# Which DMAs a kernel waits for before it ends: every semaphore, or the stores alone

## The chip, the cores and the metric

The kernel runs on one core of one Trainium2 chip. The metric is the time of one execution on the device, in microseconds; lower is better.

## The reference

Four residual layers over x of shape (1, 2048, 512) in bf16: twice a linear attention of 32 heads with softmax feature maps, each followed by a gated unit with ReLU.

```python
def reference(A_x, A_wqkv, A_w_phi, A_wo, B_x, B_W_gate, B_W_up, B_W_down):
    ...  # _A_ref: attention; _B_ref: gate * (gate > 0) * up, then W_down
    x = A_x
    x = x + _A_ref(_layernorm(x, axis=-1), A_wqkv, A_w_phi, A_wo)
    x = x + _B_ref(_layernorm(x, axis=-1), B_W_gate, B_W_up, B_W_down)
    x = x + _A_ref(_layernorm(x, axis=-1), A_wqkv, A_w_phi, A_wo)
    x = x + _B_ref(_layernorm(x, axis=-1), B_W_gate, B_W_up, B_W_down)
    return x
```

## The kernel before

A small scheduler in Python orders all operations, gives each DMA a semaphore and emits one instruction stream for each engine. Cuts are marked with `...`.

```python
    def prepare(self):
        ...
        ring = soft = 0
        for o in self.sequence:
            ...
            if o.dma:
                if e == "pool":
                    o.stream = ("d", self.n_dma_sems - 4 + soft % 4)
                    soft += 1
                else:
                    o.stream = ("d", ring % (self.n_dma_sems - 4))   # a ring of 60
                    ring += 1
                if o.stream in last_of:
                    deps.append(last_of[o.stream])
            ...
            cnt[o.stream] += 1
            o.cnt = cnt[o.stream]
        self.final = cnt

    def emit(self, e, eng, sems, dsems):
        for o in self.seq[e]:
            ...  # waits of the operation, the operation, its increment
        if e == "sp":
            for s, c in self.final.items():
                if isinstance(s, tuple) and c:
                    eng.wait_ge(dsems[s[1]], 16 * c)
```

The output leaves in 17 stores. Sixteen are issued by ScalarE's queue; the last 128 columns of the last tile are issued by SyncE:

```python
            if last:
                op(OUT_Q if w == 512 else "sp" if n0 else "act", lambda e, n0=n0, n1=n1: e.dma_start(outv[:, t:t + 1, n0:n1], x_sb[:, t:t + 1, n0:n1]), ..., dma="store", ...)
```

A wait that is written with no operation after it is attached by the compiler to the next instruction, here the branch that leaves the block. That branch keeps the first wait of the list; the others become wait instructions of up to two semaphores ahead of it, paired from the middle of the list outward, so that the list's end is waited for last. That is read from the records of this kernel: the branch carries the first of the 62 semaphores, and the last instruction the 62nd together with the second.

The softmax here doesn't subtract the row's maximum and nothing guards it: scores larger than these inputs give would overflow.

## Time and profile before

| | before |
|---|---|
| time, first three runs | 390.05, 390.68, 390.74 us |
| profiled execution: time, span | 389.32, 387.52 us |
| SyncE issues the last store | 384.80 us after the span's start |
| that store has landed | 1.51 us after its issue |
| SyncE's branch / its drain | 2.32 / 2.50 us after its issue |
| end of the span | 2.73 us after its issue |

The lower four rows are the tail; they come from the trace's single records of instructions and semaphore increments. A DMA has landed when its semaphore has had the sixteenth increment; the drain is the instruction that SyncE executes next after the branch. I measure every tail from the start of SyncE's last store issue, because that takes out whatever happened earlier in the run. The lines of the profile stand in the prediction below.

### The profile page before, as it was taken

The page shows a single profiled execution, that of the slowest core. Times are in us where ns is not written, and L with a number is a line of the kernel's source. Part 1 is how long each engine was busy: PE and PEld are TensorE (multiplying, and loading weights), DVE is VectorE, ACT ScalarE, POOL GpSimd, SP SyncE. Part 2 cuts the span into 40 slices and gives each one's busy share as a digit, 9 for nine tenths or more (in the row PEclk, how much of TensorE's full clock was granted, in tenths as well). Part 3 has the DMA queues.
Part 4 walks back from the last instruction along what each step waited for, and adds up shares of the span by engine and source line. Part 5 has one row for each costly group of instructions (what it writes and reads, how often), then busy time and mean ns, then how long its engine had stood idle before and what let it go on. Part 6 is the DMA issues. An engine that isn't in the chain of part 4 may idle for free.

```text
span 387.5 us, 6658 instructions
## 1 busy us (share of the span) xinstructions
PE 377.9 (98%) x2430; PEld 214.0 (55%) x2471; DVE 294.7 (76%) x646; ACT 195.0 (50%) x609; POOL 57.4 (15%) x129
## 2 busy tenths in 40 slices
PE   8999899999999999999999999999999999999996
PEld 7545565787554544444444467577565554454443
DVE  7999977999997886663798986899867773643442
ACT  6999859664253236243255765875343344024210
POOL 1377201213112000000000000232201020100000
PEclk9999999999999999999999999999999999999999
DMA  8451951233232222010030100022331231210101
GB/s 258 152 102 37 308 184 30 43 61 63 55 79 44 44 54 41 15 27 2 7 62 2 27 3 2 14 42 55 70 82 29 54 61 35 69 27 14 42 14 54
DMA packets 60592, 22.89 MB, mean 59 GB/s; under 512 B 51760, under 2 KB 60304, under 8 KB 60560
## 3 DMA queue, kind: packets, MB, share of 16 engines
q1 hardware_dynamic: 57440, 19.35, 22.2%
q10 hardware_dynamic: 2832, 2.08, 1.7%
q0 software_dynamic: 288, 1.05, 0.8%
q8 instruction: 19, 0.31, 0.3%
q14 instruction: 13, 0.11, 0.1%
HBM read 8.44 MB, written 2.10 MB: 27 GB/s over the span
## 4 chain that ended last, share of the span: by engine, by line
PE 76%; DVE 10%; ACT 9%; DMA 2%; issue 1%; POOL 1%; SPq 0%; POOLq 0%
PE pb L872 32%; PE pb L926 17%; PE pb L842 5%; PE pb L726 5%; PE pb L673 4%; PE pb L711 4%; PE pb L746 3%; ACT phik L684 3%; PE pb L779 3%; PE pb L900 2%; ACT expq L730 2%; PE pb L928 2%; DVE phik L702 2%; DVE stats L615 2%; DVE t L816 1%
## 5 line engine op out<-in xcount | busy, mean ns | idle before, releaser
L879 ACT ACTIVATE gate<-pb 128x512 bf16<-128x512 f32 (+1 forms) x100 | 51.0, 511 | 77.0 <-PE pb L872 74.2
L880 DVE TENSOR_TENSOR hT<-gate,pb 128x512 bf16<-128x512 bf16 (+1 forms) x100 | 56.8, 576 | 39.4 <-PE pb L872 36.9
L872 PE MATMUL pb<-yT,Wu 128*128 128x512 bf16 (+1 forms) x396 | 82.6, 336 | 0.2
L872 PE MATMUL pb<-yT,Wg 128*128 128x512 bf16 (+1 forms) x393 | 81.6, 336 | 0.5
L926 PE MATMUL pb<-Wd,hT 128*128 128x512 bf16 (+2 forms) x322 | 75.5, 372 | 0.5
L872 PEld LDWEIGHTS pb<-yT,Wu 128*128 128x128 bf16 x400 | 38.8, 98 | 30.6 <-DVE x_sb L845 0.6
L872 PEld LDWEIGHTS pb<-yT,Wg 128*128 128x128 bf16 x400 | 38.6, 98 | 29.3 <-DVE t L821 0.3
L926 PEld LDWEIGHTS pb<-Wd,hT 128*128 128x128 bf16 x330 | 31.7, 98 | 35.2
L615 DVE BATCH_NORM_STATS2 stats<-x_sb 128x6 f32<-128x512 bf16 x64 | 43.2, 686 | 1.7 <-DMA x_sb<-in_A_x_dram 1.0
L730 ACT ACTIVATE expq<-pb 128x512 bf16<-128x512 f32 x64 | 35.2, 617 | 8.9 <-PE pb L726 8.9
L684 ACT ACTIVATE phik<-pb 128x512 bf16<-128x512 f32 x64 | 35.6, 612 | 6.6 <-PE pb L673 6.6
L816 DVE TENSOR_TENSOR t<-pb,sm 128x384 bf16<-128x384 f32 x64 | 33.5, 549 | 1.4 <-POOL sm L806 1.2
L934 DVE TENSOR_TENSOR x_sb<-x_sb,pb 128x512 bf16<-128x512 bf16 (+2 forms) x33 | 21.9, 666 | 14.4 <-PE pb L928 14.4
L624 ACT ACTIVATE lnv<-mv,eps 128x1 f32<-128x1 f32 (+1 forms) x58 | 17.2, 305 | 29.7 <-DVE mv L616 29.4
L842 PE MATMUL pb<-wo,oT 128*128 128x512 bf16 x119 | 30.9, 379 | 1.0 <-DMA oT<-o 0.5
L641 DVE TENSOR_SCALAR y<-x_sb,mv,rstd 128x512 bf16<-128x512 bf16 x63 | 28.2, 462 | 4.0 <-ACT rstd L626 3.8
L711 PE MATMUL pb<-wv,yT 128*128 128x512 bf16 x124 | 30.7, 379 | 0.2
L726 PE MATMUL pb<-yT,Wqp 128*128 128x512 bf16 x124 | 30.6, 379 | 0.3
L673 PE MATMUL pb<-Wkp,yT 128*128 128x512 bf16 x120 | 30.2, 379 | 0.5 <-DMA yT<-y 0.3
L845 DVE TENSOR_TENSOR x_sb<-x_sb,pb 128x512 bf16<-128x512 bf16 x32 | 21.8, 680 | 11.3 <-PE pb L842 10.8
L793 ACT ACTIVATE sm<-pb 128x48 f32<-128x48 f32 (+1 forms) x96 | 16.5, 215 | 20.1 <-PE pb L779 19.9
L693 DVE TENSOR_REDUCE z<-phik 128x64 f32<-128x1024 bf16 x21 | 25.0, 1201 | 0.9 <-ACT phik L684 0.6
(81 smaller groups left out, 411.5 us busy)
## 6 DMA issues: line engine op xcount, KB each, us to landing
out_dram<-x_sb ACTq DMA_DIRECT2D x15, 128.0 KB, 1.7
Wg<-in_B_W_gate_dram SPq DMA_DIRECT2D x2, 640.0 KB, 6.6
Wu<-in_B_W_up_dram SPq DMA_DIRECT2D x2, 640.0 KB, 7.7
Wd<-in_B_W_down_dram SPq DMA_DIRECT2D x1, 1280.0 KB, 12.6
x_sb<-in_A_x_dram POOLq DMA_DIRECT2D x2, 512.0 KB, 4.5
yT<-y SPq DMA_TRANSPOSE x55, 2.5
Wd<-in_A_wqkv_dram SPq DMA_DIRECT2D x2, 256.0 KB, 3.0
Wd<-in_A_wqkv_dram SPq DMA_DIRECT2D x1, 512.0 KB, 5.2
```

Source lines behind the costliest of these rows:

```text
L615: op("dve", lambda e, t=t: e.bn_stats(stats[:, t, :], x_sb[:, t, :]), reads=[res("x", t)], writes=[res("st", t)], ii=600, lat=690, name=f" ...
L673: i = e.matmul(kt.ap(), src.ap()[:, ic, c0:c0 + 128], Wkp[:, ic, :], start=(ic == 0), stop=(ic == 3))
L684: op("act", lambda e, s=s: e.activation(ft.ap()[:, s, :], kt.ap(), ACT.Exp, scale=(1.0, -1.0)[s]), reads=[kr], writes=[fr2[s]], ii=477, la ...
L711: i = e.matmul(vt.ap(), src.ap()[:, ic, c0:c0 + 128], wv[:, ic, :], start=(ic == 0), stop=(ic == 3))
L726: i = e.matmul(qt.ap(), Wqp[:, ic, c * 128:(c + 1) * 128], src.ap()[:, ic, :], start=(ic == 0), stop=(ic == 3))
L730: op("act", lambda e, g=g: e.activation(es[g][0].ap(), qt.ap(), ACT.Exp, scale=(1.0, -1.0)[g]), reads=[qr], writes=[es[g][1]], ii=477, lat ...
L816: return e.tensor_tensor(tt_.ap()[:, b, 0:384].rearrange("p (c h d) -> p c h d", h=8, d=16), pt.ap()[:, 0:432].rearrange("p (c w) -> p c w ...
L842: i = e.matmul(wt.ap(), oT_.ap()[:, c, :], wo[:, c, :], start=(c == 0), stop=(c == 3))
L872: i = e.matmul(pt.ap()[:, 0:n], W[:, ic, fc * 128:(fc + 1) * 128], src.ap()[:, ic, a * 128:b * 128], start=(ic == 0), stop=(ic == 3))
L879: op("act", lambda e: e.activation(st_.ap()[:, 0:n], gt.ap()[:, 0:n], ACT.Relu), reads=[gr], writes=[sr], ii=110 + n * .72, lat=230 + n * ...
L880: op("dve", lambda e: e.tensor_tensor(ht.ap()[:, a * 128:b * 128], st_.ap()[:, 0:n], ut.ap()[:, 0:n], ALU.mult), reads=[sr, ur], writes=[h ...
L926: i = e.matmul(pt.ap()[:, 0:n1 - n0], hT[l, s, fc].ap()[:, c:c + 128], Wd[:, fc, n0:n1], start=(fc == 0), stop=False)
```

## The change

The loads and transposes have all been waited for by whoever used their data, so only the stores have nobody who waits for them. The change waits for those alone, in the order in which they are expected to land.

```diff
         if e == "sp":
-            for s, c in self.final.items():
-                if isinstance(s, tuple) and c:
-                    eng.wait_ge(dsems[s[1]], 16 * c)
+            for o in sorted((o for o in self.ops if o.dma == "store"), key=lambda o: o.end):
+                eng.wait_ge(dsems[o.stream[1]], 16 * o.cnt)
```

## The prediction

> **What bounds the kernel now.** I read the page first. TensorE is busy for 98% of the span, and the chain that ended last is made of its matmuls:
>
> ```profile
> span 387.5 us, 6658 instructions
> PE 377.9 (98%) x2430; PEld 214.0 (55%) x2471; DVE 294.7 (76%) x646; ACT 195.0 (50%) x609; POOL 57.4 (15%) x129
> ...
> PE 76%; DVE 10%; ACT 9%; DMA 2%; issue 1%; POOL 1%; SPq 0%; POOLq 0%
> ```
>
> The change touches nothing of that. It edits only the code that SyncE runs after its last DMA, so what counts is how the program ends. I therefore read the timeline from 384.4 us on (columns: start, duration, engine, line, operation):
>
> ```profile
> 383.86 0.91 DVE L934 TENSOR_TENSOR x_sb<-x_sb,pb 128x384 bf16<-128x384 bf16 x2 [1.11 <-PE pb L928]
> 384.22 0.22 PE L928 MATMUL pb<-Wd,hT 96*128 96x128 bf16 x1
> 384.45 0.34 ACTq L937 DMA_DIRECT2D out_dram<-x_sb  x1
> 384.80 0.38 SPq L937 DMA_DIRECT2D out_dram<-x_sb  x1
> ```
>
> The last matmul ends at 384.44, the last VectorE addition at 383.86 + 0.91 = 384.77, and SyncE issues the last of the 17 stores from 384.80 to 385.18. After that nothing computes, yet the span runs 2.3 us further, to 387.5. The time from issue to landing is in the list of DMA issues:
>
> ```profile
> out_dram<-x_sb ACTq DMA_DIRECT2D x1, 96.0 KB, 1.6
> out_dram<-x_sb SPq DMA_DIRECT2D x1, 32.0 KB, 1.5
> ```
>
> So the last two stores are down at about 384.45 + 1.6 = 386.1 and 384.80 + 1.5 = 386.3. In the trace's own semaphore records the sixteenth increments are at 386.08 and 386.30. The program is therefore not ended by its last store: 387.5 is 1.2 us later. Line 420 (the loop that the change replaces) and line 1001 (the end of the block) fill that stretch:
>
> ```profile
> L420 SPq EVENT_SEMAPHORE  x31: 17/28/28, 385.2 to 387.1; - x31
> ...
> L1001 SPq COMPARE_BRANCH  x1: 41/41/41, 387.1 to 387.1; - x1
> L1001 SPq DRAIN  x1: 13/13/13, 387.3 to 387.3; - x1
> ...
> L1001 DVEq DRAIN  x1: 328/328/328, 384.5 to 384.5; - x1
> L1001 ACTq DRAIN  x1: 152/152/152, 384.8 to 384.8; - x1
> ...
> L1001 POOLq EVENT_SEMAPHORE  x2: 17/17/17, 387.3 to 387.4; - x2
> L1001 SPq EVENT_SEMAPHORE  x1: 17/17/17, 387.5 to 387.5; - x1
> ```
>
> What to see: SyncE executes 31 wait instructions on one line, without a pause, from 385.2 to 387.1, then a branch and a drain; VectorE and ScalarE drained at 384.8 and 385.0. GpSimd's barrier instruction comes only after SyncE's drain, and the release of all engines ends the span. In the single records the first wait starts at 385.228, the last at 387.056, so (387.056 - 385.228) / 30 = 61 ns from one to the next, and the branch follows at 387.121. No wait in the row is longer than its neighbours: the two that carry the last stores' semaphores come up at 386.81 and 386.87, half a microsecond after those had landed. The tail is bound by SyncE's sequencer working through waits that are nearly all long satisfied.
>
> **What the Trainium skill says.** "Perfetto Trace Analysis", section "Sequencer-only Instruction (DRAIN, etc)", says that the profiler reports only the execution of such an instruction, while decode and semaphore wait lie outside. The trace agrees: 28 ns reported, 61 ns from start to start; I count with the 61. "Advanced Engine Details and Errata", section "Network/Comms", puts the reading of a semaphore by the sequencer at 50-100 ns. The records show two semaphores on 30 of the 31 instructions, so about 61 ns for two; the measurement decides. "DMA: Bandwidth & Descriptors", section "Anatomy of one DMA — SWDGE (gpsimd) path", describes about 2.0 us of fixed time, most of it the write receipt, for a software-issued DMA. These hardware-issued stores take 1.5 to 2.1 us, the last one 1.5 for 32 KB; it is the floor under the end whatever SyncE does.
>
> **The change part by part.** Removed: waits on 62 semaphores. The kernel makes 128 DMAs; SyncE and ScalarE share a ring of 60 semaphores, all used, and GpSimd's two loads have one each. 62 = 1 on the branch + 1 + 30 x 2, which is the 31 instructions plus the branch. Added: waits for the 17 stores alone. Following the kernel's own schedule (computed from the kernel before, which fixes it), the 17 stand on 17 different semaphores, so none can be merged away. By the same packing, one goes on the branch and 16 make 8 instructions. 31 - 8 = 23 instructions go; the page should count 6658 - 23 = 6635. Removed waits guard only loads and transposes, which their users wait for anyway, so the schedule of all five engines up to 385.18 is the same.
>
> The naive gain is 23 x 61 ns = 1.40 us. It can't all be had, because the landing steps in. The packing in the records is from the middle outward (first the 31st, then 32nd with 30th, and so on to the last with the second; the first in the list sits on the branch). I apply it to the 17 in the schedule's order of ends: the 16 after the first pair up from the middle, and the seventh instruction has the store that lands at 386.08, the eighth the one of 386.30. Step by step: start at 385.23 as before; six satisfied waits, 6 x 0.061, bring SyncE to 385.59; the seventh holds until 386.08; the eighth would be reached at about 386.14 and holds until 386.30. An update releases a waiting sequencer in about 0.02 us here (VectorE's last increment is at 384.78, SyncE's issue starts at 384.798), so the last wait starts at 386.32. The branch follows 0.065 later, as before (387.056 to 387.121): 386.385. Before it was 387.121, so the branch comes 0.736 us earlier. What follows (branch to drain 0.18, drain to end 0.22) is unchanged and moves with it.
>
> Sum: 1.40 us of waits removed, of which 0.66 becomes a wait for the landing; 0.74 us on the path. The profiled span should be 387.52 - 0.74 = 386.8, and the time 390.68 - 0.74 = 389.94. The three times before average 390.49, which would give 389.75; I put the point between, at 389.9.
>
> **The rivals.**
> - *The wait moves, but ends with the waits in the wrong place.* If the pairing put the last store's wait first, all seven other waits would follow its landing: 386.32 + 7 x 0.061 + 0.065 = 386.81, a gain of only 0.31 us: 390.4. For it: the order in the code is the modelled one, and the compiler permutes it. Against it: the permutation of the kernel before takes the ends of the list last, and the model's last two are the stores that landed last. The change's words promise the landing order; it needs only that the late ones come late.
> - *The landing was the end already, and the profile's row of waits is drawn out by the recording of each instruction.* Without a profile, 31 waits of 35 ns would end at 385.23 + 1.09 = 386.3 and the gain would vanish: 390.6. For it: all I have is a recorded run, and its time (389.32) is not that of the timed ones. Against it: the recorded run is the faster one, so recording does not visibly slow the kernel.
> - *The full 1.40 us*, 389.3, if the stores landed before the waits ran out. Against it: the landing at 386.30 is an event of the DMA, and the store's issue does not move.
> - *Something after the branch grows.* SyncE's program gets 23 instructions shorter and its end lies elsewhere in memory, so a late instruction fetch at the branch could eat some tenths: 390.0 to 390.4. The gap of 0.18 us between branch and drain may hold such a piece; the profile cannot say.
> - *TensorE's part changes.* Nothing in the change reaches it, but its chain is 98% of the time and 0.2% of it is as large as the gain.
>
> **Range and chances.** The mechanism can give 0 to 1.4 us, with 0.74 as the reading of the trace. The three timed runs lie 0.69 apart, as much as the gain. Adding half of that spread on either side of the point gives 389.2 to 390.6. A gain of 2% would be 7.8 us; the whole stretch from the last matmul to the end is 3.1 us, so faster by 2% is nearly excluded, and there is no added work on any path for a loss of 7.8 us. What is left, 1% each, is for a chip or state that differs.
>
> **What would show it right or wrong.** Right: the row of SyncE waits has 8 instructions instead of 31, starts at 385.2 and ends near 386.3; it has two visible stops, at the two last landings; the branch is at 386.4 and the span 386.8; every engine's busy time is as before. Wrong: a different count (packing); the last wait starting some multiples of 61 ns after the last landing (order); the branch-to-drain gap above 0.2 us (fetch); the span down 0.7 but the time not (recording). If the last stores were issued earlier or later than 384.45 and 384.80 by over 0.1 us, the difference is TensorE's, not the change's.

## The result, and the profile after

| | before | after |
|---|---|---|
| median of 6 runs | 390.19 us (389.88 to 390.74) | 389.31 us (388.85 to 389.79) |
| ratio | 1 | 0.9975, 95% interval 0.9962 to 0.9988 |
| SyncE's wait instructions | 31 | 8 |
| last store's landing after its issue | 1.505 us | 1.506 us |
| SyncE's branch after that issue | 2.323 us | 1.590 us |
| end of the span after that issue | 2.725 us | 1.993 us |

A ratio is the mean time of one kernel's fast runs over that of the other's of the same rounds, so not quite the ratio of the two medians. Here 0.9975 stands for 0.98 us; its interval, 0.47 to 1.48 us, holds the 0.73 us of the tail.

The head of the page of the kernel after, then the timeline of its end (start, duration, engine, line, operation):

```profile
span 388.0 us, 6635 instructions
```

```profile
385.65 0.34 ACTq L936 DMA_DIRECT2D out_dram<-x_sb  x1
385.99 0.38 SPq L936 DMA_DIRECT2D out_dram<-x_sb  x1
```

The wait instructions of its line 419, and the end of the block in its line 1000 (count; shortest, median and longest duration in ns; starts of the first and the last):

```profile
L419 SPq EVENT_SEMAPHORE  x8: 28/28/28, 386.4 to 387.5; - x8
```

```profile
L1000 SPq COMPARE_BRANCH  x1: 41/41/41, 387.6 to 387.6; - x1
L1000 SPq DRAIN  x1: 13/13/13, 387.8 to 387.8; - x1
```

Read against the prediction's lines: 31 has become 8, and 6658 records 6635 (both traces hold 2430 matmul records; the other eleven hold 2471). SyncE still starts to wait 0.43 us after it began to issue the last store (386.42 against 385.99). In the single records six waits follow each other at 59 to 74 ns, the seventh starts only with the landing of the last store but one, the eighth 16 ns after the last landing, and the branch 68 ns later.

But this profiled run's span is longer than the one of before, 387.99 against 387.52. The last store is issued 1.2 us later, and that happened at the beginning of the run. These are the transfers of the query weights in the two lists of DMA issues (size, time to landing), before and then after:

```profile
Wd<-in_A_wqkv_dram SPq DMA_DIRECT2D x1, 512.0 KB, 5.2
```

```profile
Wd<-in_A_wqkv_dram SPq DMA_DIRECT2D x1, 512.0 KB, 7.3
```

In the timeline of after the first transposes of these weights had to wait for them, and VectorE's second copy of the group after the transposes; the same copy in the timeline of before is the second fence:

```profile
10.49 0.62 PE L586 MATMUL pb<-ident,Wd 128*128 128x128 bf16 x8 [1.46 <-DMA Wd<-in_A_wqkv_dram]
...
10.92 0.42 DVE L477 COPY yT<-pb 128x512 bf16<-128x512 bf16 x1 [1.31 <-PE pb L586]
```

```profile
9.53 0.42 DVE L478 COPY yT<-pb 128x512 bf16<-128x512 bf16 x1
```

Is that the change's doing? Nothing before SyncE's last store differs in the two programs, and the 13 traces, in which that part of the program is the same but for one kernel that adds waits in SyncE's idle time, show the copy anywhere between 9.22 us and 10.92 us. In eleven of them it starts 0.48 us after the query weights have landed; in the two with the earliest landings (before and one_each) 1.20 and 0.57 us pass. Why the landings vary is not shown. From the copy to the last store's issue it is then 374.95 to 375.27 us in twelve of the traces. The thirteenth, order_alone, has 376.39 us; there the granted TensorE clock (a share of full speed) is 0.50 from 11 to 14 us, and 1.00 in the same window of all the others. So the arrival of the first loads spreads the times by more than the change moves them, and each tail has to be read by itself.

### The profile page after: what moved, and what is told of

It reads as the page before. It is cut to its first block, busy times and chain, and to the rows that moved or that the text cites. A ratio compares the mean times of both kernels' runs of the same rounds, so it can differ in the third digit from the quotient of the medians.

```text
span 388.0 us, 6635 instructions
## 1 busy us (share of the span) xinstructions
PE 378.6 (98%) x2430; PEld 214.7 (55%) x2471; DVE 294.8 (76%) x646; ACT 194.9 (50%) x609; POOL 57.3 (15%) x129
## 4 chain that ended last, share of the span: by engine, by line
PE 78%; ACT 9%; DVE 8%; DMA 2%; issue 1%; SPq 1%; POOL 1%; POOLq 0%
PE pb L871 33%; PE pb L925 17%; PE pb L841 5%; PE pb L725 5%; PE pb L672 4%; PE pb L710 4%; PE pb L745 3%; ACT phik L683 3%; PE pb L778 3%; PE pb L899 2%; DMA Wd<-in_A_wqkv_dram 2%; ACT expq L729 2%; PE pb L927 2%; DVE phik L701 2%; ACT vaug L476 1%
```

## The experiments

**Theory A.** SyncE takes about 61 ns for each wait instruction, satisfied or not, and these 31 instructions outlast the landing of the last store. The change takes 23 away; the gain is cut off where the landing becomes the end. The rivals are named in the expectations. All runs were correct and timed in five rounds against the kernel before. "Tail" is from SyncE's issue of the last store to its branch. The first four kernels shared a chip and the runs of before (median 390.28 us), the next four (390.06) and the last three (389.76) likewise. Three runs of before in the last two groups (391.97, 392.27 and 392.01 us) show a mean granted clock of 0.995 or 0.996 and are 1.9 to 2.5 us longer than the median of their group. They make the ratios of these seven kernels rougher; their tails do not depend on them.

### after_again: the changed kernel once more

No edit.

> The changed kernel once more, on the same chip as the next three. The tail is measured from SyncE's issue of the last store to its branch: 2.32 us in the trace of before, 1.59 in that of after. Theory A (each wait instruction costs SyncE 61 ns until the landing takes over; nothing else changed): tail 1.59 again, time 0.73 us lower than before, ratio 0.998. Rival B (part of the 0.88 us between the two medians comes from the rest of the kernel): the time falls by about 0.9 to 1.0 again with the tail still 1.59, and the loads at the start land earlier in most runs.

Measured: tail 1.590 us; 389.65 us, ratio 0.9980 (0.9968 to 0.9992), that is 0.78 us. The tail is the same to the nanosecond, and the time has moved less than in the first comparison. The interval of the gain, 0.31 to 1.25 us, holds both A's 0.73 and rival B's 0.9 to 1.0, so the time does not decide between them. The trace gives no sign of a second gain: the copy came late here, at 10.75 us.

### order_alone: 62 waits in another order

```diff
+            st = sorted((o for o in self.ops if o.dma == "store"), key=lambda o: o.end)
+            late = {o.stream: o.cnt for o in st}
+            rest = {s: c for s, c in self.final.items() if isinstance(s, tuple) and c and s not in late}
-            for s, c in self.final.items():
-                if isinstance(s, tuple) and c:
-                    eng.wait_ge(dsems[s[1]], 16 * c)
+            for s, c in list(rest.items()) + list(late.items()):
+                eng.wait_ge(dsems[s[1]], 16 * c)
```

> All 62 waits as before, only their order changed: the others first, then the stores in the order of landing, so the last store's wait is the last of the 31 instructions. Theory A (the count makes the tail; no wait of before ever blocks): tail 2.32, time as before, ratio 1.000. Rival C (the order makes the gain, because before waits for the stores in the wrong place): tail about 1.6, ratio 0.998.

```profile
L422 SPq EVENT_SEMAPHORE  x31: 17/28/28, 387.3 to 389.1; - x31
```

Measured: tail 2.323 us, that of before to the nanosecond; 390.37 us, ratio 1.0002 (0.9989 to 1.0015). Again 31 instructions in 1.83 us without a stop. Rival C is out: order alone gives nothing, because in a row that outlasts the landing no wait ever blocks.

### count_alone: the 17 stores in the order of their semaphores' numbers

```diff
+            kept = {o.stream for o in self.ops if o.dma == "store"}
             for s, c in self.final.items():
-                if isinstance(s, tuple) and c:
+                if s in kept:
                     eng.wait_ge(dsems[s[1]], 16 * c)
```

> Only the 17 stores' waits, but in the order of the semaphores' numbers as before; the last store's wait comes in the fourth of 8 instructions. Theory A: the fourth holds until the landing (1.50 after the issue), then four more and the branch: 1.50 + 0.02 + 4 x 0.061 + 0.065 = 1.83 us of tail, 0.49 less than before and 0.24 more than after. Rival D (the count alone makes the gain, order counts for nothing): tail 1.59.

```profile
L421 SPq EVENT_SEMAPHORE  x8: 27/28/889, 386.3 to 387.6; - x8
```

Measured: tail 1.803 us, 0.52 less than before and 0.21 more than after; 389.63 us, ratio 0.9979 (0.9966 to 0.9992). The fourth instruction ends 22 ns after the landing, and four more follow. So 0.52 of the 0.73 us comes from the count alone, and 0.21 needs the order as well; rival D is out. The times of this run and of after_again cannot be told apart; the tails can.

One thing to see in the line: the fourth instruction is recorded with 889 ns. It waits for two semaphores, and the one named first in its record is long satisfied while the second is the last store's. In the kernel after, the first-named one is the late one, and all durations are 28 ns.

### dose_124: 124 satisfied waits more

```diff
         if e == "sp":
+            for k in range(1, 125):
+                eng.wait_ge(sems["pe"], k)
             for s, c in self.final.items():
```

> As before, with 124 more waits that have long been satisfied (on TensorE's counter), 93 instructions instead of 31. Theory A: 62 x 0.061 = 3.78 us more: tail 6.10, time 390.2 + 3.8 = 394.0, ratio 1.0097. Rival E (satisfied waits cost nothing or little in the time, and the gain of the change comes from elsewhere): ratio under 1.004.

```profile
L419 SPq EVENT_SEMAPHORE  x31: 17/28/28, 386.2 to 388.0; - x31
L422 SPq EVENT_SEMAPHORE  x62: 28/28/28, 388.1 to 391.8; - x62
```

Measured: tail 6.104 us; 393.61 us, ratio 1.0089 (1.0076 to 1.0102), that is 3.5 us. From 31 to 93 instructions the tail grew by 3.78 us, 61 ns each, on waits that nothing held up. Rival E is out: satisfied waits are paid in the measured time of the execution, not only in the trace. (The dose's interval is 3.0 to 4.0 us, so the time confirms the price to about a seventh. Whether a run without any recording would pay the same is taken up below.)

### branch_last: the last store's wait on the branch

```diff
+            st = sorted((o for o in self.ops if o.dma == "store"), key=lambda o: o.end)
-            for o in sorted((o for o in self.ops if o.dma == "store"), key=lambda o: o.end):
+            for o in st[-1:] + st[:-1]:
```

> As after, with the last store's wait first in the code, so that the branch itself carries it and the eighth instruction carries the store before it. Theory A: the eighth holds until 1.28 us after the issue, the branch until 1.50 + 0.02: tail 1.53 instead of 1.59, too little for the time to show (0.06 us, 0.02%). Rival F (the branch needs its usual 0.065 us after the landing anyway, or holds longer than a wait instruction): tail 1.59 or more.

```profile
L420 SPq EVENT_SEMAPHORE  x8: 28/28/28, 386.0 to 386.9; - x8
```

```profile
L1001 SPq COMPARE_BRANCH  x1: 41/41/41, 387.1 to 387.1; - x1
```

Measured: tail 1.519 us, 17 ns after the landing; 389.15 us, ratio 0.9970 (0.9949 to 0.9990). The branch starts 17 ns after its own semaphore is met, so rival F is out. The 0.07 us shows in the trace only.

### last_first: the two last stores waited for first

```diff
+            st = sorted((o for o in self.ops if o.dma == "store"), key=lambda o: o.end)
-            for o in sorted((o for o in self.ops if o.dma == "store"), key=lambda o: o.end):
+            for o in st[:8] + st[-2:] + st[8:-2]:
```

> The 17 waits of after, with the two last stores' waits in the first of the 8 instructions. Theory A: it holds until the landing at 1.50, then seven more instructions and the branch: 1.50 + 0.02 + 7 x 0.061 + 0.065 = 2.01 us of tail; of the gain of 0.73 only 0.31 is left. Rival D (order counts for nothing): 1.59.

```profile
L420 SPq EVENT_SEMAPHORE  x8: 28/28/28, 386.9 to 387.4; - x8
```

Measured: tail 2.042 us; 389.63 us, ratio 0.9988 (0.9966 to 1.0011). The first of the eight starts 1.53 us after the store's issue, and the seven others and the branch follow it. This is the price of a wrong order with the same count: 0.45 us of the 0.73. Rival D is out here too, by the trace; the interval of the ratio holds 1.

### hidden_14: 14 satisfied waits beside the landing

```diff
-            for o in sorted((o for o in self.ops if o.dma == "store"), key=lambda o: o.end):
-                eng.wait_ge(dsems[o.stream[1]], 16 * o.cnt)
+            st = sorted((o for o in self.ops if o.dma == "store"), key=lambda o: o.end)
+            late = {o.stream for o in st}
+            more = [s for s in self.final if isinstance(s, tuple) and self.final[s] and s not in late][:14]
+            for s, c in [(o.stream, o.cnt) for o in st[:1]] + [(s, self.final[s]) for s in more] + [(o.stream, o.cnt) for o in st[1:]]:
+                eng.wait_ge(dsems[s[1]], 16 * c)
```

> As after, with 14 further satisfied waits, each paired with a store's, so 15 instructions, the last two stores still last. Theory A: 13 satisfied ones take 0.43 + 13 x 0.061 = 1.22 us, less than the 1.28 of the last store but one, so they lie beside its flight: tail 1.59 as after. Rival G (each instruction costs 61 ns wherever it stands): 1.59 + 7 x 0.061 = 2.02.

```profile
L422 SPq EVENT_SEMAPHORE  x15: 28/28/28, 385.7 to 386.8; - x15
```

Measured: tail 1.580 us with 15 instructions, as with 8; 389.02 us, ratio 0.9972 (0.9951 to 0.9993). Waits that run while the last store flies are free, and rival G is out. This is also why the change could not get the whole 1.40 us.

### one_each: one semaphore in each instruction

```diff
             for s, c in list(rest.items()) + list(late.items()):   # as order_alone
                 eng.wait_ge(dsems[s[1]], 16 * c)
+                eng.nop(nofuse=True)
```

The no-operation takes the wait, so nothing is left over to be paired; what arrives in the program are 62 wait instructions.

> All 62 waits, stores last, but one semaphore in each instruction: 62 instead of 31. Theory A in its form of a cost per instruction: 31 x 0.061 = 1.89 us more than before: tail 4.21, ratio 1.0048. Rival H (the cost is that of reading a semaphore, about 30 ns each): tail 2.3, ratio 1.000.

```profile
L423 SPq EVENT_SEMAPHORE  x62: 17/17/17, 384.7 to 387.7; - x62
```

```profile
L1004 SPq DRAIN  x1: 7/7/7, 387.8 to 387.8; - x1
```

Measured: last wait 3.470 us and drain 3.527 us after the issue (before: 2.258 and 2.500); 390.91 us, ratio 1.0014 (0.9993 to 1.0035). Both theories fail. An instruction with one semaphore takes 49.6 ns from start to start (384.840 to 387.716 over 58 of them), one with two takes 61. So neither the instruction nor the semaphore alone sets the price: in these programs one costs about 50 ns, a second in the same instruction about 11 more.

The run showed a second thing that I had not looked for: the drain comes 57 ns after the last wait, not 65 + 177 as in before. Here the branch carries no wait and leaves no record. The next two kernels test that.

### branch_free: the changed kernel with no wait on the branch

```diff
+            st = sorted((o for o in self.ops if o.dma == "store"), key=lambda o: o.end)
-            for o in sorted((o for o in self.ops if o.dma == "store"), key=lambda o: o.end):
+            for o in st[-1:] + st[:-1]:
                 eng.wait_ge(dsems[o.stream[1]], 16 * o.cnt)
+            eng.nop(nofuse=True)
```

> The 17 waits, the last store's in the last of 9 wait instructions, and none on the branch (a no-operation ahead of the branch takes it). In the run with one semaphore in each instruction the branch carried no wait, left no record, and SyncE's drain followed its last wait's start by 57 ns; with a wait on the branch that is 65 + 177 = 242 ns. Theory K (a wait on the branch costs some 0.18 us of its own): from the last store's issue to SyncE's drain 1.59 us, against 2.50 in before, 1.77 in after and about 1.69 with the last store on the branch; time 0.91 us under before, ratio 0.9977. Rival L (the 0.18 us is a fetch of the instructions after the branch, wait or no wait, and was short there for another reason): 1.77.

```profile
L420 SPq EVENT_SEMAPHORE  x8: 17/28/28, 385.6 to 386.5; - x8
L421 SPq EVENT_SEMAPHORE  x1: 27/27/27, 386.7 to 386.7; - x1
```

```profile
L1002 SPq DRAIN  x1: 7/7/7, 386.8 to 386.8; - x1
```

Measured: drain 1.587 us after the issue, against 1.767 in after and 2.500 in before; 388.91 us, ratio 0.9972 (0.9952 to 0.9992). Rival L is out: with nothing else altered behind it, the step from branch to drain has all but gone. This kernel has the shortest tail of all, 0.18 us under the changed kernel, but the two were not timed side by side and 0.18 us is less than these times can tell.

### branch_free_62: the kernel before with no wait on the branch

```diff
                     eng.wait_ge(dsems[s[1]], 16 * c)
+            eng.nop(nofuse=True)
```

> All 62 waits in the order of before, 31 instructions of two semaphores, none on the branch. Theory K: last wait 2.26 us after the last store's issue as before, drain 0.06 after that: 2.32 instead of 2.50; time 0.18 us under before, ratio 0.9995, which five rounds can't tell from 1. Rival L: 2.50.

```profile
L421 SPq EVENT_SEMAPHORE  x1: 28/28/28, 387.9 to 387.9; - x1
```

```profile
L1002 SPq DRAIN  x1: 7/7/7, 387.9 to 387.9; - x1
```

Measured: last wait 2.264 us, drain 2.329 us after the issue; 389.81 us, ratio 0.9993 (0.9972 to 1.0014), from which the time shows nothing. The 0.17 us is there with 62 waits too, so it belongs to the branch and not to the number of waits.

### waits_early: 56 of the 62 waits where SyncE idles

```diff
+            if e == "sp" and o is self.seq[e][-1]:
+                st = sorted((q for q in self.ops if q.dma == "store"), key=lambda q: q.end)
+                late = {q.stream for q in st[-6:]}
+                for s, c in self.final.items():
+                    if isinstance(s, tuple) and c and s not in late:
+                        eng.wait_ge(dsems[s[1]], 16 * c)
             ins = o.fn(eng)
 ...
         if e == "sp":
-            for s, c in self.final.items():
-                if isinstance(s, tuple) and c:
-                    eng.wait_ge(dsems[s[1]], 16 * c)
+            for o in sorted((o for o in self.ops if o.dma == "store"), key=lambda o: o.end)[-6:]:
+                eng.wait_ge(dsems[o.stream[1]], 16 * o.cnt)
```

> All 62 waits are kept, but 56 of them stand before SyncE's last store, where SyncE idles for 33.8 us (28 instructions); after the store come three instructions and the branch for the last six stores. Theory A: nothing of the 28 is on the path, the last store is issued as soon after its data as before (18 ns after VectorE's increment), tail to the branch 1.59 as after, ratio 0.998. Rival M (waits cost wherever they stand, or hold the store back): the last store comes up to 1.7 us late, ratio 1.000 or more.

```profile
L417 SPq EVENT_SEMAPHORE  x28: 27/28/28, 352.0 to 365.1; - x28
L425 SPq EVENT_SEMAPHORE  x3: 17/28/28, 386.2 to 387.3; - x3
```

Measured: tail 1.593 us, the last store issued 17 ns after VectorE's increment as in before; 389.53 us, ratio 0.9979 (0.9955 to 1.0002). All 62 waits are made and the tail is that of the changed kernel. Rival M is out by the trace (the interval of the ratio just holds 1): what cost time was where the waits stood.

### The tails side by side

| kernel | wait instructions after the last store | to the branch, us | to the drain, us |
|---|---|---|---|
| before | 31 | 2.323 | 2.500 |
| order_alone | 31 | 2.323 | 2.500 |
| branch_free_62 | 31 | no record | 2.329 |
| last_first | 8 | 2.042 | 2.219 |
| count_alone | 8 | 1.803 | 1.980 |
| after, after_again | 8 | 1.590 | 1.767 |
| hidden_14 | 15 | 1.580 | 1.757 |
| waits_early | 3 | 1.593 | 1.770 |
| branch_last | 8 | 1.519 | 1.696 |
| branch_free | 9 | no record | 1.587 |

From the drain to the end of the span it is 0.21 to 0.23 us in every trace, and the last store lands 1.50 to 1.51 us after its issue.

## Why the prediction was right or wrong

- **What bounds the end: right.** The row of satisfied waits did. order_alone, dose_124 and waits_early show it from three sides.
- **The counts: right.** 31 became 8. The record count fell by 23 as forecast, but that match is partly luck: both traces hold 2430 matmul records where the other eleven hold 2471, and after_again, the same kernel, counts 6676. No engine's busy time changed by more than 0.8 us.
- **61 ns for each instruction: right** for instructions with two semaphores, 61.0 ns over the 62 that dose_124 adds. As a price of an instruction as such it is wrong: with one semaphore it is 50. The prediction's sum did not need that.
- **How much becomes a wait for the landing: right.** Predicted 0.736 us earlier at the branch, measured 2.323 - 1.590 = 0.733. hidden_14 shows the slack that swallows the rest of the 1.40 us.
- **The order of the waits: right.** In the code's order and the compiler's pairing the last two landings come last. (The prediction counts the pairing's places one too low; by the records it is the 32nd alone, then the 33rd with the 31st. Nothing in its sum hangs on it.) count_alone and last_first show what a wrong order costs: 0.21 and 0.45 us. The first rival's 0.31 us of remaining gain was 0.28 in last_first.
- **The span of 386.8 us: wrong in the profiled run**, which had 387.99. The step that failed is "the schedule of all five engines up to 385.18 is the same": the order was, but the last store was issued at 385.99. The prediction laid such a shift to TensorE in advance; it was the first loads, 7.3 instead of 5.2 us for the query weights, and TensorE waited for them. Without the shift of 1.20 us the span would have been 386.79.
- **The time: in the range, which by itself shows little.** 389.31 us lies 0.6 us under the point. Most of that is the kernel before, which measured 390.19 us over six runs and not the 390.5 to 390.7 that I had begun from: 390.19 - 0.74 is 389.45, and the 0.14 that remains is within the interval of the comparison. The range was also not what its own working gives: half of the spread of 0.69 us on either side of 389.9 is 389.55 to 390.25, which would have missed 389.31; the range written down is the whole spread on either side. And it is so wide that the kernel before, at 390.19, lies in it. That the time fell inside is therefore partly luck; what confirms the sum is the tail.
- **The rival of a recorded run that exaggerates: not borne out, not closed.** The dose appears in the time at 3.5 us where the trace has 3.78, with an interval that holds both. Every timed run also came with a span, 1.8 us under its time, so none of them shows a kernel that was not recorded. For the same reason the prediction's argument against this rival, that the recorded run was the faster one, says little.
- **"Something after the branch grows": it did not.** The 0.18 us from branch to drain that "the profile cannot say" anything about goes away when no wait is put on the branch. Whether that is the wait itself or the form that the branch then takes (a record of a compare-and-branch appears only with it) stays open.

## What to carry to other kernels

When nothing computes after the last store, read single records from its issue to the end: if wait instructions keep starting at even steps after the last landing, the program ends with bookkeeping. Wait at the end only for what nobody else has waited for, place the last landing in the last wait, and do other waits while an engine idles or a store is in flight, where they are free. Before crediting a gain of 0.2% to a change, measure the changed stretch from a mark inside the same trace; here the landing of the first loads alone moved the last store's issue by more than twice as much.

## What the Trainium skill lacked or had wrong

- "Perfetto Trace Analysis", section "Sequencer-only Instruction (DRAIN, etc)", puts the semaphore wait outside the reported time. That held for the semaphore named first in a record. Where the second-named one was late, the wait was inside: 889 ns instead of 28 in count_alone, and in the trace of before nine wait instructions of TensorE's queue with two semaphores, recorded with 199 to 1681 ns, each end 34 or 35 ns after the last increment of the second-named (one with nothing to wait for: 51 ns). The measurement decides. The page also gives no price; here it was 50 ns from start to start with one semaphore and 61 with two.
- "Advanced Engine Details and Errata", section "Network/Comms", gives 50-100 ns for the reading of a semaphore. A whole wait instruction with one semaphore took 50 ns, the bottom of that range, and a second semaphore only 11 ns more.
- The same page, section "Control Flow Timing", gives about 51 ns for a branch and 108 ns for a compare-and-branch. Here a branch with a wait was recorded as a compare-and-branch of 41 ns with 159 to 177 ns from its start to the next instruction; one without a wait left no record, and the drain came 57 to 65 ns after the start of the last wait. No page says that a wait on the block's last branch costs this.
- No page was found that prices a row of satisfied waits at a kernel's end: 1.83 us for 31 instructions here, of which 0.73 us could be taken off the tail.
